# Attention and a token mixer on one core: the quarter-product form of the first mixer product for three groups of tokens instead of two, with the mixer's work spread thinner over attention

## The chip, the cores and the metric

The kernel runs on one core of one Trainium2 chip. The metric is the device time of one execution in microseconds (us). Several executions are timed; the time quoted is their median. A profile is one execution recorded instruction by instruction; its engines are TensorE (PE, and PEld for its weight loads), VectorE (DVE), ScalarE (ACT), GpSimd (POOL) and SyncE (SP, which only issues transfers). A line such as L650 is a line of the kernel's source.

## The reference

```python
# attention: batch 8, heads 8, sequence 576, head dimension 64
scores = q @ k^T / 8
cum    = cumsum(max(s, 0))                     # per batch and head
scores = where(causal, -1e9, scores + min(-(cum_row - cum_col), 0))
attn   = softmax(scores)
x      = (attn @ v)                            # as [batch, 576, 512]
# mixer over the sequence, of rank 32, and over the channels
u   = x + (x^T @ U @ V)^T
out = u + max(u @ w_ch1, 0) @ w_ch2            # 512 -> 2048 -> 512
```

Inputs and outputs are float32; the kernel multiplies in bfloat16 and accumulates in float32.

## The kernel before

**Attention.** The 64 (batch, head) pairs are taken two at a time, so there are 32 head pairs n, four for each batch b. For a head pair, `transposes` (L317) turns q and k on TensorE and copies them into one of a few `slot` tiles; `scores` (L404) makes the transposed scores in `pscore` banks, ScalarE takes the exponential into a `pT` tile (L419, L430), VectorE masks the diagonal (L349); `values` (L464) multiplies by v, and VectorE divides by the row sums into `x_sb` (L473, L474). From batch 2 on, SP also transposes x_sb into xT by a transfer (L481).

**Sequence mixer.** When a batch's four pairs are done, `seqmix` makes u for it. It is a chain between TensorE and VectorE: x by U (L493), a copy to uxT (L502), a transpose (L506), a copy to ux (L508), ux by V for the first 512 tokens (L538) and for the last 64 (L563). VectorE then adds xT and writes u transposed into the tiles `uT` (L518, up to seven pieces).

**Channel mixer.** The 4608 tokens of all batches are cut into nine groups g of 512, so a group reaches over two batches: group 6 is complete with batch 6, groups 7 and 8 only with batch 7, the last. `chanmix(g)` makes the first product `hidden` (L650): 16 steps of four matmuls of 512 columns, each followed by a ReLU on ScalarE into hT (L1018). Then `outputs_by_quarters` makes the second product with seven quarter products instead of eight (Strassen's scheme in Winograd's form): seven products of two times eight matmuls of 256 columns (L699), sums of the weights made once, sums of quarters of hT (`total` L677, the first of them by `first_sums`), and additions into the output tiles (L713). From group NG - 3 = 6 on, `outputs_by_quarters` uses fewer PSUM banks of its own (`quarter`, tags y and z), which exist only in the tail.

**Weaving.** TensorE's order is the order of the program. A list `fill` holds generators of mixer work; `step_fill` takes one unit (for the products, mostly four matmuls of L650 or eight of L699) whenever the counter `pace[0]` passes 16, and `pace[1]` is added at every step of attention. The pace is 12 of 16 from batch 3 to 5 and 10 of 16 after. `chanmix(b - 1)` joins the list in the second head pair of batch b, right after seqmix(b - 1). When group 6's first product is finished, `step_fill` does nothing until the tail's PSUM pools exist. VectorE's, ScalarE's and SP's order after batch 0 is decided by the scheduler, except that weight sums are held behind the VectorE instruction recorded ahead of them (`placed`).

**Tail.** After attention, groups 7 and 8 take the quarter-product form for the first product too: `hidden_by_quarters` (L929) needs sums of the weights w1 (`first_weight_sums`, eight VectorE instructions at L899) and of u (`token_sums`, L911 to L914). Four sets e of seven products of 2x2 matmuls of 256 columns are made per group, with copies and ReLUs on ScalarE (L965, L976, L979, L983, L944, L948) and additions on VectorE (L942). The weight sums lie in the slots that attention leaves free, so they can't be made before its last pairs; here they are stepped one by one inside group 6's `chanmix`. The second product of the group before is woven in by hand: the tuple `fills` says after which step how many units run. The last sequence mixer, seqmix(7), is run by this loop, whose `fill_with` calls place first-product units of group 6 between its steps:

```python
if b == B:
    fill_with(3)
    for _ in range(3):
        step(mixing)
        fill_with(2)
...
for _ in mixing:
    fill_with(1)
```

Of the kernel before, what the change touches and what calls it, by code (L numbers as in the profile page):

```python
# [13 lines left out]
BF16 = mybir.dt.bfloat16  # L14
# [25 lines left out]
def kernel(  # L40
# [17 lines left out]
    DM = H * D  # L58
# [6 lines left out]
    PB = NP // B  # L65
# [2 lines left out]
    KA = D + 4  # L68
    NF = FF // 128
    FT = 2  # L70

    consts = ctx.enter_context(tc.tile_pool(name="consts", bufs=1))
    loads = ctx.enter_context(tc.tile_pool(name="loads", bufs=2))
# [50 lines left out]
    def ones(ap):  # L124
        nc.vector.memset(ap.bitcast(mybir.dt.uint32), 0x3F803F80)

    busy = consts.tile([128, 512], BF16)
    ones(busy)

    alloc_qk(0)  # L130
# [4 lines left out]
    load_qk(0, 4, 2)  # L135
    load_qk(0, 6, 2)

    sel = consts.tile([128, 516], BF16)
    nc.vector.memset(sel, 0.0)
    nc.gpsimd.affine_select(  # L140
        out=sel,
# [102 lines left out]

    w1_sb = consts.tile([128, 4, FF], BF16)
    w2_sb = consts.tile([128, NF, DM], BF16)
    HF, HD = NF // 2, DM // 2
    B11, B21, B22 = w2_sb[:, :HF, :HD], w2_sb[:, HF:, :HD], w2_sb[:, HF:, HD:]
    B12 = w2_sb[:, :HF, HD:]
    B_1, B_2, B_4 = (consts.tile([128, HF, HD], BF16, name=f"w2_sum{i}") for i in (1, 2, 4))  # L250
    B_3 = B12

    def weight_sums():
# [29 lines left out]

    def uT(g):
        if g not in uT_of:
            uT_of[g] = work.tile([128, 4, 512], BF16, tag="uT", name="uT", bufs=3)
        return uT_of[g]


# [299 lines left out]
        for j, pv in enumerate(pvs):  # L589
            nc.vector.tensor_copy(vt[:, j, :, 0:D], pv.rearrange("p (h d) -> p h d", h=H))  # L590

    ux_first = work.tile([128, PB, 128], BF16, tag="ux_first", name="ux_first", bufs=1)

    def mix_first(dt, copy):
        x_sb = x_of[0]
# [89 lines left out]
    def outputs_by_quarters(g, hT, u_sd):  # L685
# [324 lines left out]
    def chanmix(g, hT=None, done=0):  # L1010
        u = uT_of.pop(g)
        if g > 0:
            hT = work.tile([128, NF, 512], BF16, tag="hT", name="hT")
            sums = {1: weight_sums, NG - 3: first_weight_sums}.get(g, lambda: iter(()))()
        for nf in range(done, NF):
            f1 = pwork()
            hidden(f1, u, nf, range(4))
            nc.scalar.activation(hT[:, nf, :], f1, RELU)  # L1018
            if g > 0:
                next(sums, None)  # L1020
            if g > 0 and nf in (12, 14):
                first_sums(hT, nf == 12)
            if nf == (3 if g > 0 else NF - 1):
                u_sd = by_token(u)
            if nf == NF - 1:
                expanded.append(g)
            yield
        if g > 0:
            yield from outputs_by_quarters(g, hT, u_sd)
            return  # L1030
        ahead = {}
        if g == 0:
            for i in range(2):
                ahead[i] = pwork()
                for _ in outputs(ahead[i], hT, i, range(8)):
                    yield
                yield
        for i in range(4):
            f2 = ahead[i] if i in ahead else pwork()
            for _ in outputs(f2, hT, i, range(8 if i in ahead else 0, NF)):  # L1040
                yield
            o_sb = work.tile([128, DM], FP32, tag="o_sb", name="o_sb", bufs=3)
            nc.vector.tensor_tensor(
                o_sb.rearrange("p (a b) -> p a b", a=4),
                f2.rearrange("p (a b) -> p a b", a=4),
                u_sd[:, :, i, :],
                op=ALU.add,
            )
            nc.sync.dma_start(out=out_flat[ds(g * 512 + i * 128, 128), :], in_=o_sb)
            yield  # L1050
# [165 lines left out]
    for n in range(2 * PB, NP + 2):  # L1216
# [36 lines left out]
    tail_sums = {}  # L1253
    tail_sums[NG - 2] = token_sums(
        uT(NG - 2), v_slots[1].rearrange("p a b c -> p (a b c)")
    )
    xT_again = work.tile([128, 4, 640], BF16, tag="xT", name="xT", bufs=1)
    def hidden_plain(u, hT, nfs):
        for at, nf in enumerate(nfs):
            f1 = pwork()  # L1260
# [1 line left out]
            nc.scalar.activation(hT[:, nf, :], f1, RELU)  # L1262
            yield

    for g, sets, fills in ((NG - 2, 4, (0, 0, 2, 4, 6, 8, 10, 12, 14, 17, 20, 23, 25, 26)), (NG - 1, 4, (1, 3, 5, 7, 9, 11, 13, 16, 19, 22, 25, 25, 26, 26))):
        u = uT_of.pop(g)
        u_sd = by_token(u, True)
        hT = work.tile([128, NF, 512], BF16, tag="hT", name="hT")
        for at, _ in enumerate(hidden_by_quarters(u, tail_sums[g], hT, sets)):
            for _ in range(fills.count(at)):  # L1270
                step_fill()
            if at == 3 and g < NG - 1:
                tail_sums[NG - 1] = token_sums(
                    uT(NG - 1), xT_again.rearrange("p a b -> p (a b)")
                )
        if sets < 4:
            for one in (True, False):
                first_sums(hT, one)
# [36 lines left out]
```

## Time and profile before

| | |
|---|---|
| time, median of 3 runs | 363.01 us (362.35 to 363.12) |
| span of the profiled execution, first to last instruction | 362.1 us |
| TensorE busy | 350.2 us, 97% |
| VectorE busy | 276.5 us, 76% |
| ScalarE busy | 213.0 us, 59% |
| first products, L650 | 401 recorded matmuls of 512 columns |
| TensorE's granted clock, mean | 1.000 |

The span covers the instructions; the listed times of the runs are up to 1.0 us longer, which is what lies around them. A row of the timeline gives the start from the span's start, the length, the engine, the line, and the tiles as output<-inputs; the length of a matmul includes its pipeline, so what one costs in a stream is read from the distance of starts. A few matmul records are missing from the trace, so counts can fall one short. In a row of the windows the columns are the window, its length, then busy time and number of instructions of PE, PEld, DVE, ACT and POOL, the granted clock, the share of the transfer engines and GB/s.

### The profile page before, as it was taken

To read this page: it belongs to the slowest core of one execution; us is meant where nothing else is said; L and a number is where in the kernel's file an instruction comes from. 1 tells how busy PE (TensorE), PEld (TensorE's weight loads), DVE (VectorE), ACT (ScalarE), POOL (GpSimd) and SP (SyncE) were. 2 spreads that over 40 slices of the span, in tenths; PEclk is the share of its full clock that TensorE was granted. 3 is DMA by queue.
4 is the path that set the end of the run, shared out by engine and by line. 5 is a ranking of instruction groups with operands and counts; after the bars stand their busy time and mean duration, and the time that the engine had idled before them with its cause. 6 is when DMAs were issued, how large, how long until landed. Compare 5 with 4: busy or idle time off the path is not lost.

```text
span 362.1 us, 9616 instructions
## 1 busy us (share of the span) xinstructions
PE 350.2 (97%) x3999; PEld 256.7 (71%) x4039; DVE 276.5 (76%) x605; ACT 213.0 (59%) x322; POOL 84.7 (23%) x108
## 2 busy tenths in 40 slices
PE   8999999999998999999999999999899999999996
PEld 3676566665587667876688667876488548888885
DVE  8776776778788758995699659986697769676674
ACT  3875975846761678347843676348743554675710
POOL 8997261714040403140214013000000000000000
PEclk9999999999999999999999999999999999999999
DMA  7999999999999899969994999255022716010022
GB/s 104 169 198 204 150 174 129 152 150 143 98 109 114 147 121 70 97 94 126 128 91 72 127 150 91 51 123 79 4 38 70 143 24 125 29 60 31 30 89 87
DMA packets 155123, 37.94 MB, mean 105 GB/s; under 512 B 138696, under 2 KB 153448, under 8 KB 155080
## 3 DMA queue, kind: packets, MB, share of 16 engines
q0 software_dynamic: 110016, 18.50, 82.6%
q1 hardware_dynamic: 44776, 18.64, 31.4%
q8 instruction: 31, 0.51, 0.6%
q10 hardware_dynamic: 288, 0.20, 0.2%
q14 instruction: 12, 0.10, 0.1%
HBM read 37.25 MB, written 9.70 MB: 130 GB/s over the span
## 4 chain that ended last, share of the span: by engine, by line
PE 76%; DVE 11%; ACT 4%; DMA 4%; issue 3%; POOL 1%; DVEq 0%; ACTq 0%; POOLq 0%
PE pwork L650 21%; PE pwork L699 11%; PE pscore L404 9%; PE quarter L699 9%; PE pwork L464 7%; PE parts L929 6%; PE pwork L317 4%; PE pwork L660 3%; DMA xT<-x_sb 2%; DVE slot L677 2%; DVE uT L518 2%; ACT hT L1018 2%; DVE o_sb L713 2%; DMA k_sd<-in_k_dram 2%; ACT pT L419 1%
## 5 line engine op out<-in xcount | busy, mean ns | idle before, releaser
L650 PE MATMUL pwork<-uT,w_sb 128*128 128x512 bf16 x401 | 105.9, 379 | 2.6 <-ACT hT L1018 0.9
L1018 ACT ACTIVATE hT<-pwork 128x512 bf16<-128x512 f32 x108 | 65.2, 608 | 38.4 <-PE pwork L650 38.2
L419 ACT ACTIVATE pT<-pscore 128x1024 bf16<-128x1024 f32 x56 | 56.5, 1029 | 49.8 <-PE pscore L404 49.0
L650 PEld LDWEIGHTS <-w_sb 128*128 128x128 bf16 x448 | 38.3, 98 | 35.9 <-issue 1.3
L404 PE MATMUL pscore<-slot 68*128 68x320 bf16 (+1 forms) x500 | 55.2, 246 | 0.2
L404 PEld LDWEIGHTS <-slot 68*128 68x128 bf16 x564 | 41.2, 97 | 16.9 <-issue 1.3
L699 PEld LDWEIGHTS <-hT 128*128 128x128 bf16 x496 | 46.3, 98 | 7.0 <-DVE uT L518 0.5
L188 POOL DMA_DIRECT2D v_slot<-in_v_dram x36 | 30.3, 855 | 77.6 <-PE pwork L464 65.9
L349 DVE TENSOR_TENSOR pT<-pT,keep 128x512 bf16<-128x512 bf16 (+1 forms) x81 | 28.6, 354 | 21.8 <-ACT pT L419 16.0
L337 DVE COPY slot<-pwork 64x576 bf16<-64x576 bf16 x76 | 34.4, 453 | 4.6 <-PE pwork L317 3.7
L464 PEld LDWEIGHTS <-pT 128*128 128x128 bf16 x870 | 32.4, 98 | 6.9 <-issue 1.8
L464 PE MATMUL pwork<-v_slot,pT 128*128 128x65 bf16 x870 | 35.5, 193 | 1.2 <-DVE uT L518 1.2
L474 DVE TENSOR_TENSOR x_sb<-pwork,rec 128x320 bf16<-128x320 f32 x64 | 31.2, 488 | 1.4
L430 ACT ACTIVATE pT<-pscore 128x1024 bf16<-128x1024 f32 x29 | 30.2, 1043 | 1.7 <-PE pscore L404 1.5
L699 PE MATMUL pwork<-w_sb,hT 128*128 128x256 bf16 x240 | 30.6, 273 | 0.0
L340 DVE COPY slot<-pwork 64x576 bf16<-64x576 bf16 x29 | 23.3, 802 | 5.4 <-PE pwork L317 3.6
L699 PEld LDWEIGHTS <-slot 128*128 128x128 bf16 x256 | 24.1, 98 | 4.6 <-issue 1.6
L114 POOL DMA_DIRECT2D q_sd<-in_q_dram x6 | 12.6, 2105 | 47.2 <-PE pwork L317 34.5
L473 DVE RECIPROCAL rec<-pwork 128x5 f32<-128x5 f32 x64 | 12.0, 190 | 12.3 <-PE pwork L464 12.1
L699 PE MATMUL pwork<-w_sum,slot 128*128 128x256 bf16 x160 | 20.3, 272 | 0.7 <-DVE o_sb L713 0.7
L317 PEld LDWEIGHTS <-q_sd 72*128 72x128 bf16 x256 | 14.7, 98 | 8.8 <-DMA q_sd<-in_q_dram 1.0
L699 PE MATMUL quarter<-w_sb,hT 128*128 128x256 bf16 x144 | 18.0, 273 | 0.3 <-DVE uT L518 0.3
(165 smaller groups left out, 544.4 us busy)
## 6 DMA issues: line engine op xcount, KB each, us to landing
out_dram<-o_sb SPq DMA_DIRECT2D x34, 256.0 KB
w_sb<-in_moe_w_ch_dram POOLq DMA_DIRECT2D x4, 1024.0 KB, 14.3
v_slot<-in_v_dram POOLq DMA_DIRECT2D x28, 128.0 KB, 8.3
q_sd<-in_q_dram POOLq DMA_DIRECT2D x5, 576.0 KB, 15.6
k_sd<-in_k_dram POOLq DMA_DIRECT2D x5, 576.0 KB, 21.8
q_sd<-in_q_dram POOLq DMA_DIRECT2D x4, 288.0 KB, 13.2
k_sd<-in_k_dram POOLq DMA_DIRECT2D x4, 288.0 KB, 13.5
q_sd<-in_q_dram POOLq DMA_DIRECT2D x4, 144.0 KB, 5.2
```

The costliest lines, as they stand in the source:

```text
L188: nc.gpsimd.dma_start(out=vt[:rows_t, t, :, 0:D], in_=v[b, :, ds(t * 128, rows_t), :].rearrange("h p d -> p h d"),)
L317: nc.tensor.transpose(tps[hh][:, c, t2, :], src[:, 2 * hp + hh, ds(t2 * 128, 128)], identity[:TP, :TP],)
L337: copies(n, hh, par)(by_run[:, :, :, par, :], src)
L349: nc.vector.tensor_tensor(dst, dst, keep[:, :, 0:w].to_broadcast([128, n_tiles, w]), op=ALU.min)
L404: nc.tensor.matmul(dst, lhsT=slot[0:KA, hh, ds(S + j * 128, 128)], rhs=slot[0:KA, hh, lo:hi], start=True, stop=True,)
L419: nc.scalar.activation(pT[:, hh, 0:1024], near, EXP, scale=scale)
L430: nc.scalar.activation(pT[:, :, 1024:1536], mid.rearrange("p (a b) -> p a b", a=2), EXP, scale=scale)
L464: nc.tensor.matmul(po[:, i, :], lhsT=pT[:, hh, ds(place(j, i), 128)], rhs=vt[:, j, h, :], start=(j == 0), stop=(j == i), skip_group_check= ...
L474: nc.vector.tensor_tensor(x_sb[:, hp, :, ds(hh * D, D)], po[:, :, 0:D], rec.to_broadcast([128, 5, D]), op=ALU.mult,)
L650: nc.tensor.matmul(f1, lhsT=w1_sb[:, kt, ds(nf * 128, 128)], rhs=u[:, kt, :], start=(kt == 0), stop=(kt == 3),)
L699: nc.tensor.matmul(acc[:, i, :], lhsT=a[:, kt, ds(i * 128, 128)], rhs=b[:, kt, :], start=(begin and i == 0 and kt == 0), stop=(kt == HF - ...
L1018: nc.scalar.activation(hT[:, nf, :], f1, RELU)
```

## The change

A name GL = NG - 4 = 5 is introduced. The groups after GL, that is 6, 7 and 8, take the quarter-product form of the first product in the tail; `chanmix` runs for groups up to 5 in attention. Group 5's second product moves to the tail's form of `outputs_by_quarters`, and `step_fill` now stops when group 5's first product is finished. The pace is 9 of 16 throughout from batch 3 on. The eight weight sums of w1 are made after the attention loop, one before each of eight calls of `step_fill`. The uT tiles are four, not three; to make room, three small tiles of the start (`busy`, `sel`, `ux_first`) are placed inside the tiles that later hold the sums of w2.

```diff
+    GL = NG - 4
...
-    busy = consts.tile([128, 512], BF16)
+    HF, HD = NF // 2, DM // 2
+    B_1, B_2, B_4 = (consts.tile([128, HF, HD], BF16, name=f"w2_sum{i}") for i in (1, 2, 4))
+    busy = B_1.rearrange("p k n -> p (k n)")[:, 0:512]
...
-    sel = consts.tile([128, 516], BF16)
+    sel = B_2.rearrange("p k n -> p (k n)")[:, 0:516]
...
-            uT_of[g] = work.tile([128, 4, 512], BF16, tag="uT", name="uT", bufs=3)
+            uT_of[g] = work.tile([128, 4, 512], BF16, tag="uT", name="uT", bufs=4)
...
-    ux_first = work.tile([128, PB, 128], BF16, tag="ux_first", name="ux_first", bufs=1)
+    ux_first = B_4.rearrange("p k n -> p (k n)")[:, 0:512].rearrange("p (a b) -> p a b", a=PB)
...
-            if g < NG - 3:
+            if g < GL:
...
-        if g >= NG - 3:
+        if g >= GL:
...
-            sums = {1: weight_sums, NG - 3: first_weight_sums}.get(g, lambda: iter(()))()
+            sums = weight_sums() if g == 1 else iter(())
...
-        if NG - 3 in expanded and not ps_tail:
+        if GL in expanded and not ps_tail:
...
-            fill.append(chanmix(b - 1))
-            pace[1] = 12 if b < 6 else 10
+            if b - 1 <= GL:
+                fill.append(chanmix(b - 1))
+            pace[1] = 9
...
     pace[1] = 16
-    while NG - 3 not in expanded:
+    sums = first_weight_sums()
+    for _ in sums:
+        step_fill()
+    while GL not in expanded:
         step_fill()
...
-    tail_sums[NG - 2] = token_sums(
-        uT(NG - 2), v_slots[1].rearrange("p a b c -> p (a b c)")
-    )
+    sum_tiles = [v_slots[1].rearrange("p a b c -> p (a b c)")]
+    tail_sums = {GL + 1: token_sums(uT(GL + 1), sum_tiles[0])}
     xT_again = work.tile([128, 4, 640], BF16, tag="xT", name="xT", bufs=1)
+    sum_tiles.append(xT_again.rearrange("p a b -> p (a b)"))
...
-    for g, sets, fills in ((NG - 2, 4, (0, 0, 2, ...)), (NG - 1, 4, (1, 3, 5, ...))):
+    sets = 4
+    for g in range(GL + 1, NG):
+        if g == GL + 1:
+            fills = (0, 0, 2, 4, 6, 8, 10, 12, 14, 17, 20, 23, 25, 26)
+        else:
+            fills = (1, 3, 5, 7, 9, 11, 13, 16, 19, 22, 25, 25, 26, 26)
...
-                tail_sums[NG - 1] = token_sums(
-                    uT(NG - 1), xT_again.rearrange("p a b -> p (a b)")
-                )
+                tail_sums[g + 1] = token_sums(uT(g + 1), sum_tiles[(g - GL) % 2])
```

More of the change, by code (lines that the diff above doesn't have):

```diff
@@ L246 @@
     w2_sb = consts.tile([128, NF, DM], BF16)
-    HF, HD = NF // 2, DM // 2
     B11, B21, B22 = w2_sb[:, :HF, :HD], w2_sb[:, HF:, :HD], w2_sb[:, HF:, HD:]
     B12 = w2_sb[:, :HF, HD:]
-    B_1, B_2, B_4 = (consts.tile([128, HF, HD], BF16, name=f"w2_sum{i}") for i in (1, 2, 4))
     B_3 = B12
@@ L1252 @@
     ps_t = ctx.enter_context(tc.tile_pool(name="ps_t", bufs=4, space=bass.MemoryType.PSUM))
-    tail_sums = {}
-    tail_sums[NG - 2] = token_sums(
-        uT(NG - 2), v_slots[1].rearrange("p a b c -> p (a b c)")
-    )
+    sum_tiles = [v_slots[1].rearrange("p a b c -> p (a b c)")]
+    tail_sums = {GL + 1: token_sums(uT(GL + 1), sum_tiles[0])}
     xT_again = work.tile([128, 4, 640], BF16, tag="xT", name="xT", bufs=1)
+    sum_tiles.append(xT_again.rearrange("p a b -> p (a b)"))
     def hidden_plain(u, hT, nfs):
@@ L1263, in hidden_plain @@
             yield
-    for g, sets, fills in ((NG - 2, 4, (0, 0, 2, 4, 6, 8, 10, 12, 14, 17, 20, 23, 25, 26)), (NG - 1, 4, (1, 3, 5, 7, 9, 11, 13, 16, 19, 22, 25, 25, 26, 26))):
+    sets = 4
[4 more added lines that the diff above has]
+            fills = (1, 3, 5, 7, 9, 11, 13, 16, 19, 22, 25, 25, 26, 26)
         u = uT_of.pop(g)
```

## The prediction

> **What bounds the kernel now.** I read the page first (busy time, slices, chain), then the windows by stage, then the timeline of TensorE and of VectorE around the place where attention hands over to the mixer's tail.
>
> ```profile
> PE 350.2 (97%) x3999; PEld 256.7 (71%) x4039; DVE 276.5 (76%) x605; ACT 213.0 (59%) x322; POOL 84.7 (23%) x108
> ...
> PEclk9999999999999999999999999999999999999999
> ...
> PE 76%; DVE 11%; ACT 4%; DMA 4%; issue 3%; POOL 1%; DVEq 0%; ACTq 0%; POOLq 0%
> ```
>
> TensorE is busy for 97% of the span, at full clock throughout, and it carries 76% of the chain that ended last. So a matmul saved is worth its spacing in the stream, as long as no wait takes its place.
>
> The windows (length, then busy time of PE, PEld, DVE, ACT, POOL) show how much room the other engines have:
>
> ```profile
> 221.00:240.00 19.00, 18.59 (x251) 16.39 (x250) 18.26 (x42) 6.70 (x11) 0.00 (x0) 1.00 0.58 66
> 240.00:263.00 23.00, 21.82 (x251) 13.46 (x254) 15.75 (x41) 17.41 (x29) 0.00 (x0) 1.00 0.37 62
> 321.00:346.00 25.00, 25.00 (x230) 22.26 (x229) 17.22 (x28) 15.37 (x25) 0.00 (x0) 1.00 0.11 38
> ```
>
> Where attention is woven with second products (221 to 240) VectorE is at 96%; where it is woven with first products (240 to 263) ScalarE is at 76% and TensorE idles 1.2 us; in the tail (321 to 346) TensorE never idles. Over 122 to 281 TensorE's idle time adds up to 2.7 us.
>
> The handover, TensorE's timeline (start, us, then the instructions):
>
> ```profile
> 289.13 0.65 PE L493 MATMUL pwork<-U_sb,x_sb 128*128 128x32 bf16 x20
> 289.64 1.89 PE L650 MATMUL pwork<-uT,w_sb 128*128 128x512 bf16 x8
> 291.36 0.22 PE L506 MATMUL pwork<-identity,uxT 128*128 128x128 bf16 x1
> 291.42 1.89 PE L650 MATMUL pwork<-uT,w_sb 128*128 128x512 bf16 x7
> 293.24 0.39 PE L538 MATMUL pscore<-V_sb,ux 32*128 32x512 bf16 x2
> ...
> 293.57 2.76 PE L650 MATMUL pwork<-uT,w_sb 128*128 128x512 bf16 x12
> 296.44 0.29 PE L563 MATMUL pwork<-V_end,ux 128*128 128x64 bf16 x4
> 296.57 0.60 PE L929 MATMUL parts<-uT,w_sb 128*128 128x256 bf16 x4
> 297.44 1.92 PE L699 MATMUL quarter<-w_sb,hT 128*128 128x256 bf16 x16 [0.26 <-DVE uT L518]
> 299.19 0.60 PE L929 MATMUL parts<-v_slot,slot 128*128 128x256 bf16 x4
> ```
>
> And VectorE's:
>
> ```profile
> 281.50 2.49 DVE L899 TENSOR_TENSOR slot<-w_sb 128x1024 bf16<-128x1024 bf16 x4
> ...
> 286.11 0.49 DVE L474 TENSOR_TENSOR x_sb<-pwork,rec 128x320 bf16<-128x320 f32 x1
> ...
> 291.62 0.29 DVE L508 CAST ux<-pwork 128x128 bf16<-128x128 f32 x1 [1.50 <-PE pwork L506]
> ...
> 294.44 1.28 DVE L518 TENSOR_TENSOR uT<-pscore,xT 128x128 bf16<-128x128 f32 x2
> 295.64 1.74 DVE L518 TENSOR_TENSOR uT<-pwork,xT 128x64 bf16<-128x64 f32 x5
> ```
>
> The reader is to see that the last sequence mixer (L493, L506, L538, L563) is a chain of round trips to VectorE, and that 27 wide matmuls of L650 are shown inside it as cover (44 from 285.68 on, by the built order); and that VectorE makes its eight weight sums (L899) under that cover, from 281.5 to 288.4.
>
> **The sum, part by part.** *The products.* Group 6 goes from 64 matmuls of 512 columns to 7x4x4 = 112 of 256; the built programs differ by exactly these 48. Wide ones: eight from 289.64 to 291.36, 0.2155 us each, so 64 take 13.79. Narrow ones: sixteen from 297.44 to 299.19, 0.109 each, so 112 take 12.2. Saved: **1.6 us** on TensorE, all of it on the path.
>
> Here a rule speaks against the change. The Trainium skill's page "TensorE: Matmul & The Clock Gate", section "Back-to-back issue gap", gives about 131 ns a matmul for 512 columns in a real stream with weight loads and 81 for 128; its isolated formula is columns over 2.4 GHz plus 2.5 ns. By the stream figures, with an estimate of 98 ns between them for 256, 64 cost 8.4 us and 112 cost 10.9, a loss of 2.6. The rows above go by the isolated formula, weight loads included, so I keep the gain.
>
> *The handover.* In the built order of the new kernel group 5's first product is used up too early: nine units of four wide matmuls run ahead of attention's last values, one between the two heads, two after them, then TensorE has L493, L506, L538, L563 with nothing between, and then the tail. VectorE's order behind them is: seven pieces of L518, all eight L899, the second half of one token total (L677), one add of L942, the first o_sb of group 5 (L713). TensorE's waits in that order: the first L929 on the pair's pieces of L518, the first L699 on the last piece, the next L929 on the first two L899, a later one on six of them, and the third kind of quarter product (A_2 by B_2) on that o_sb. I put zero where the last values matmuls have streamed (285.68 in the old trace) and use the old rows:
> - x_sb is done at 1.25 (0.92 in the old trace, plus 0.33 for a token sum that now stands between). xT's transfer: its packets ended at 289.42, 2.8 after the x_sb of 286.60; with issue and semaphore, 4.3 here.
> - Eight wide matmuls to 1.73, L493 (0.51) to 2.24. VectorE then has two token sums and a total first, uxT ends at 2.85; L506 at 2.95; ux (0.26 after it starts, 0.29 long, as at 291.36 and 291.62) ends at 3.55; L538 and L563 to 4.1.
> - L518 starts when xT is there, 4.35; the pair is done 1.28 later, all 2.94 later (294.44 to 297.38). So the first L929 goes at 5.7 and the first sixteen L699 at 7.35, ending 9.1.
> - Eight L899, 0.60 apart (four in 2.49), end at 12.1; three more at 0.60 end at 13.9. A_2 by B_2 can start at **14.0**.
> - What TensorE streams up to there: 1.72 + 0.51 + 0.06 + 0.33 + 0.12 + 0.44 + 1.75 + five eights of 0.87 = 9.3. Lost: 4.7 us.
>
> The old trace loses in the same stretch: 303.56 - 285.68 = 17.9 against 17.0 streamed, 0.85. Net 3.9; and VectorE, which was 3 us ahead there, now starts the tail level: its next eleven instructions (7x0.60 + 4x0.33 = 5.5) stand against six eights (5.2), 0.3 more. **Cost 4.2 us.** Bounds: 2.0 if xT, evacuation and sums overlap better than their order says (only the idle before the first L699 remains), 5.5 if VectorE stays late through the group, which at 17.22 of 25 us busy it need not.
>
> A slow clock could follow such idling. The trace shows half speed only at its start: nine matmuls of 512 columns in 4.02 us, 0.43 each, where 0.2155 each would make 1.9. In its middle, 1.1 us without a matmul (256.7 to 257.8) left the spacing at 0.215; the idle stretches reckoned here are 1.6 and 1.2 us. So I take nothing, and 2.0 us as the upper bound, one such start. The same page, section "What's actually happening", has the clock fall to half after an idle window of some 3.4 us; by that too nothing is lost unless the stretches count as one.
>
> *Attention with 9 units in 16 steps, not 12 or 10.* About 4.5 units per head pair, not 6 or 5. TensorE per pair: 2.9 (16 L317, 18 of L404, 30 L464 at their spacings) plus 4.5x0.87 = 6.8, against 8.0 seen at pace 12 and 7.1 at pace 10. The moved units themselves cost the same in the tail. What changes is cover. The slices at pace 10 (221 to 281) idle 1.6 us in 60, those at pace 12 (122 to 221) 1.0 in 99, and 0.9 of the former is one wait of L650 for L1018 where a sequence mixer fell among first products. In the new order two of five fall so (b = 4, 5), in the old one such; the stage is some 26 us shorter. I take **0**: bounds -1.5 (over half the idle goes) and +3 (next part).
>
> *At nothing.* Group 5's second products take the tail's form: seven wide adds on VectorE, not eleven; the matmuls are the same. Its sends and u_sd transposes stand in SP's order behind the same xT transposes. The third tail group's x_sb is the one that group 6 leaves, 24 us before it is read. The DMA issues on POOL come earlier with attention: q and k for the next batch landed 18 us before use (218.5 for 236.8), a batch of four pairs gets some 6 us shorter, so this cover holds; without it, each us late is one lost. The fourth uT only adds memory. The shared tiles: last read by matmuls at about 21 (busy), 20 (sel) and 34 us (ux_first), first sum at 77.
>
> Sum: -1.6 + 4.2 + 0 = +2.6. The span was 362.1 and the median of the runs 363.0, 0.9 lies around the span: 364.7 in the span, **365.7 us** as a time.
>
> **Rivals.** *Attention gives back more than the handover takes* (the faster side): with fewer units VectorE falls below saturation in the second-product stretches and ScalarE in the others, and TensorE's 2.7 us of idle there, and the small gaps beside it, go. For it: 96% on VectorE. Against: TensorE lost only 0.4 us in that very window. At the handover's lower bound: -1.6 + 2.0 - 1.5 = -1.1, 361.9. It decides from where attention's gain passes the handover's cost less 1.6.
>
> *VectorE becomes attention's bound.* Per pair it needs about 3.3 us at its spacings, 0.8 for its share of the sequence mixer, and 0.74 per second-product unit: 4.5 units make 7.4 against TensorE's 7.1 with its mixer share. Over some 12 such pairs 3.6 us: 369.3. Against: the lag is caught up among first products, as now.
>
> *The clock falls at the handover:* 365.7 + 2.0 = 367.7. Against: the idle stretches are short.
>
> **How the numbers follow.** The forecast has 0.6, the faster rival 0.15, VectorE 0.15, clock 0.1. The range reaches from the faster rival's time to the VectorE rival's, 361.9 to 369.3. No change means within 0.2% (0.7 us), about what a measurement of this kernel can tell: faster 0.17 (the faster rival and a rest of the forecast), same 0.08, slower 0.75.
>
> **What would show it.** Right: L929 at about 0.109 spacing in three groups, L650 with 64 fewer; at the handover a wait of TensorE of over 1 us on uT L518 and waits on the sums' line, the clock at 1.00. Wrong: no idle there, or idle spread over attention, or VectorE's second-product windows at 100% with TensorE below 95%.

## The result, and the profile after

The changed kernel is slower: 374.85 us (median of six runs, 373.33 to 379.58) against 363.05 us for the kernel before on the same chip, a ratio of 1.030 with a 95% interval of 1.026 to 1.035. The forecast was 365.7 us, with a range up to 369.3. The profiled execution, the quickest, took 373.33 us with a span of 371.6; the others had a mean granted clock as low as its 0.995 or lower (down to 0.976), and the ratio leaves out two of them, of 379.2 and 379.6 us, that fell into a slower state of the chip. In the changed kernel the lines named here are numbered one higher than before: L651 is the wide first product, L700 the second product, L930 the quarter form of the first, L519 the writing of u, L900 makes the weight sums, and L678 and L714 are what L677 and L713 were.

The page of the changed kernel, with the busy times, the clock in 40 slices and the chain that ended last:

```profile
PE 355.9 (96%) x4087; PEld 263.4 (71%) x4087; DVE 281.2 (76%) x617; ACT 217.6 (59%) x329; POOL 85.0 (23%) x108
...
PEclk9999999999999999999999999999998999999999
...
PE 64%; DVE 15%; ACT 9%; DMA 6%; issue 4%; SPq 1%; ACTq 0%; DVEq 0%
```

TensorE's share of the chain fell from 76% to 64%, VectorE's and ScalarE's rose by 4 and 5 points, and one slice has a clock below full. The windows of the changed kernel (length, then PE, PEld, DVE, ACT, POOL, granted clock) say in which stages:

```profile
221.00:240.00 19.00, 18.17 (x235) 12.30 (x233) 14.17 (x36) 14.69 (x24) 0.00 (x0) 1.00 0.11 22
240.00:258.00 18.00, 17.11 (x240) 14.87 (x237) 16.09 (x37) 6.89 (x10) 0.00 (x0) 1.00 0.47 93
273.00:279.00 6.00, 3.85 (x54) 2.20 (x52) 6.00 (x17) 1.79 (x3) 0.00 (x0) 1.00 0.51 30
279.00:289.00 10.00, 8.93 (x65) 7.23 (x66) 10.00 (x21) 2.77 (x5) 0.00 (x0) 0.83 0.28 53
289.00:312.00 23.00, 23.00 (x213) 20.57 (x211) 18.91 (x33) 15.11 (x24) 0.00 (x0) 1.00 0.14 47
```

From 273 to 289, the handover, VectorE is busy without a gap and TensorE idles 3.2 us; from 289 on TensorE is full again. In attention TensorE idles some 5% in both kinds of stretch (0.8 us of 19 beside first products, 0.9 of 18 beside second ones; before, 1.2 of 23 and 0.4 of 19), although VectorE is busy for 75% of the first stretch and 89% of the second, ScalarE for 77% and 38%.

Where the time went can be counted at one mark, the prediction's zero: the start of the wide matmuls right behind attention's last values. It moved from 285.68 to 273.62 us, 12.06 earlier. But 112 quarter matmuls of group 5 (12.2 us) and 28 wide ones (6.03) fewer stand ahead of it, so it should have come 18.2 earlier: attention lost **6.2 us**. Behind the mark the span grew by 21.56, and the work there by 16.65 (two times 112 narrow matmuls more, 24.4, and 36 wide ones fewer, 7.76): handover and tail lost **4.9 us**. Less the products' 1.6, which are reckoned here from the same distances of starts, this is the growth of the span, 9.5.

The handover on TensorE in the changed kernel (start, length, instruction, and in brackets the wait):

```profile
273.62 1.89 PE L651 MATMUL pwork<-uT,w_sb 128*128 128x512 bf16 x8
275.34 0.66 PE L494 MATMUL pwork<-U_sb,x_sb 128*128 128x32 bf16 x20
276.62 0.23 PE L507 MATMUL pwork<-identity,uxT 128*128 128x128 bf16 x1 [0.62 <-DVE uxT L503]
277.24 0.39 PE L539 MATMUL pscore<-V_sb,ux 32*128 32x512 bf16 x2 [0.39 <-DVE ux L509]
...
279.04 0.61 PE L930 MATMUL parts<-uT,w_sb 128*128 128x256 bf16 x4 [1.18 <-DVE uT L519]
280.68 2.95 PE L700 MATMUL quarter<-w_sb,hT 128*128 128x256 bf16 x16 [1.04 <-DVE uT L519]
283.43 1.06 PE L930 MATMUL parts<-v_slot,slot 128*128 128x256 bf16 x4
...
288.46 1.04 PE L700 MATMUL quarter<-w_sum,slot 128*128 128x256 bf16 x8
```

The first L930 stands at zero + 5.4 and the sixteen L700 at zero + 7.1 (predicted 5.7 and 7.35). But these sixteen need 2.75 us to the next start, not 1.75, and the last row, A_2 by B_2, starts at zero + 14.84 without a wait. The same kernel's granted clock, microsecond by microsecond, shows why:

```profile
280.00:281.00 1.00, 0.32 (x3) 0.29 (x3) 1.00 (x3) 0.31 (x1) 0.00 (x0) 1.00 0.01 3
281.00:282.00 1.00, 1.00 (x9) 0.77 (x7) 1.00 (x3) 0.00 (x0) 0.00 (x0) 0.68 1.09 209
282.00:283.00 1.00, 1.00 (x6) 0.70 (x5) 1.00 (x3) 0.00 (x0) 0.00 (x0) 0.50 1.16 217
283.00:284.00 1.00, 1.00 (x6) 0.75 (x5) 1.00 (x3) 0.00 (x0) 0.00 (x0) 0.50 0.52 96
284.00:285.00 1.00, 1.00 (x8) 0.73 (x7) 1.00 (x3) 0.00 (x0) 0.00 (x0) 0.61 0.00 0
```

For some 3.4 us TensorE ran at half speed, just when its work had come: 0.32 + 0.50 + 0.50 + 0.39 = 1.7 us. VectorE in the same stretch of the changed kernel:

```profile
277.70 1.28 DVE L519 TENSOR_TENSOR uT<-pscore,xT 128x128 bf16<-128x128 f32 x2
278.90 1.73 DVE L519 TENSOR_TENSOR uT<-pwork,xT 128x64 bf16<-128x64 f32 x5
280.55 2.48 DVE L900 TENSOR_TENSOR slot<-w_sb 128x1024 bf16<-128x1024 bf16 x4
...
286.57 0.68 DVE L714 TENSOR_TENSOR o_sb<-quarter,u_sd 128x512 f32<-128x512 f32 x1
```

The order is the predicted one: u, the weight sums, then the first o_sb, which ends at 287.25. TensorE, slowed by its clock, came to the product that needs it only at 288.46, so the waits that were predicted behind the sums did not happen; the half clock stood in their place. Without its 1.7 us TensorE would have come at about 286.8 (an estimate), half a microsecond before that end.

The list of TensorE's waits in attention of the changed kernel (86 to 273 us: waiter, tile, releaser, then total us, times, longest):

```profile
PE pwork L651 <- ACT hT L1019: 1.8, 2, 0.9
PE pwork L494 <- DVE x_sb L475: 1.1, 2, 0.6
PE pwork L651 <- DVE x_sb L475: 1.0, 4, 0.4
PE pwork L700 <- DVE x_sb L475: 0.8, 2, 0.5
PE pwork L651 <- DVE o_sb L714: 0.6, 1, 0.6
PE pwork L465 <- DVE uT L519: 0.5, 1, 0.5
```

The same list of the kernel before (86 to 285 us):

```profile
PE pwork L464 <- DVE uT L518: 1.2, 1, 1.2
PE pwork L650 <- ACT hT L1018: 0.9, 1, 0.9
PE pwork L699 <- DVE o_sb L713: 0.7, 2, 0.4
PE pwork L650 <- DVE x_sb L474: 0.2, 1, 0.2
```

Only the first and the last two kinds have a counterpart of any size there. The products do not read x_sb, so their waits on it are for a PSUM bank: it still holds values that VectorE has not divided and copied out. L494 does read x_sb: of its two waits the first (0.6 us) is for the bank that it writes, the second (0.5) for the last head pair's values themselves.

### The profile page after: what moved, and what is told of

Its sections match the earlier page's. It is cut to its first block, busy times and chain, and to the rows that moved or that the text cites. A ratio compares the mean times of both kernels' runs of the same rounds, so it can differ in the third digit from the quotient of the medians.

```text
span 371.6 us, 9775 instructions
## 1 busy us (share of the span) xinstructions
PE 355.9 (96%) x4087; PEld 263.4 (71%) x4087; DVE 281.2 (76%) x617; ACT 217.6 (59%) x329; POOL 85.0 (23%) x108
## 4 chain that ended last, share of the span: by engine, by line
PE 64%; DVE 15%; ACT 9%; DMA 6%; issue 4%; SPq 1%; ACTq 0%; DVEq 0%
PE pwork L651 14%; PE quarter L700 13%; PE parts L930 9%; PE pwork L700 7%; PE pscore L405 6%; PE pwork L465 4%; DMA xT<-x_sb 4%; ACT pT L420 4%; PE pwork L661 3%; PE pwork L318 3%; ACT hT L1019 3%; DVE o_sb L714 2%; DVE uT L519 2%; DVE slot L678 2%; ACT pT L431 2%
## 5 line engine op out<-in xcount | busy, mean ns | idle before, releaser
L651 PE MATMUL pwork<-uT,w_sb 128*128 128x512 bf16 x368 | 91.9, 379 | 3.7 <-ACT hT L1019 1.8
L1019 ACT ACTIVATE hT<-pwork 128x512 bf16<-128x512 f32 x92 | 55.7, 611 | 35.6 <-PE pwork L651 35.3
L651 PEld LDWEIGHTS <-w_sb 128*128 128x128 bf16 x384 | 33.1, 98 | 34.4 <-issue 3.6
L405 PE MATMUL pscore<-slot 68*128 68x320 bf16 (+1 forms) x500 | 53.4, 246 | 0.5 <-DMA slot<-hT 0.3
L700 PEld LDWEIGHTS <-hT 128*128 128x128 bf16 x496 | 47.2, 99 | 9.2 <-issue 1.7
L465 PE MATMUL pwork<-v_slot,pT 128*128 128x65 bf16 x870 | 34.1, 194 | 0.6 <-DVE uT L519 0.5
L700 PEld LDWEIGHTS <-slot 128*128 128x128 bf16 x256 | 24.0, 98 | 3.9 <-issue 0.7
L700 PE MATMUL quarter<-w_sb,hT 128*128 128x256 bf16 x192 | 25.3, 280 | 1.0 <-DVE uT L519 1.0
L700 PE MATMUL pwork<-w_sb,hT 128*128 128x256 bf16 x192 | 24.6, 273 | 0.5 <-DVE x_sb L475 0.4
L943 DVE TENSOR_TENSOR hT<-pT,parts 128x512 bf16<-128x512 f32 x24 | 16.2, 684 | 9.9 <-PE parts L930 7.1
```

The source lines that it names most:

```text
L405: nc.tensor.matmul(dst, lhsT=slot[0:KA, hh, ds(S + j * 128, 128)], rhs=slot[0:KA, hh, lo:hi], start=True, stop=True,)
L465: nc.tensor.matmul(po[:, i, :], lhsT=pT[:, hh, ds(place(j, i), 128)], rhs=vt[:, j, h, :], start=(j == 0), stop=(j == i), skip_group_check= ...
L651: nc.tensor.matmul(f1, lhsT=w1_sb[:, kt, ds(nf * 128, 128)], rhs=u[:, kt, :], start=(kt == 0), stop=(kt == 3),)
L700: nc.tensor.matmul(acc[:, i, :], lhsT=a[:, kt, ds(i * 128, 128)], rhs=b[:, kt, :], start=(begin and i == 0 and kt == 0), stop=(kt == HF - ...
```

## Experiments: which part costs what

Five kernels. The first four ran beside the kernel before at a median of 363.25 us, the last on another chip.

**The pace alone.** In the kernel before:

```diff
-            pace[1] = 12 if b < 6 else 10
+            pace[1] = 9
```

> The kernel before, with the pace of 9 from batch 3 on and nothing else of the change: two groups in the tail, the old weight sums inside group 6's first product, and the work that attention leaves over run densely around seqmix(7). Theory 1 (thin cover: with 4.5 units per head pair TensorE waits for PSUM banks and sequence mixers inside attention): about 5 us slower than before, 368, and the idle time of TensorE up to the last values matmul is about 11 us as in the changed kernel, against 6 before. Rival (attention's extra idle comes from something else in the change, such as the fourth uT or the moved sums): 363, no change.

370.78 us, ratio 1.021 (1.019 to 1.023), clock 1.000. Most of the loss is in this one number, which the prediction had priced at nothing. TensorE's waits in its attention are those of the changed kernel to within 0.3 us in each row.

**Units kept for the last sequence mixer.** In the changed kernel, whose fill_with calls ran in both rounds of the last batch:

```diff
-        if b == B:
+        if n == NP + 1:
             fill_with(3)
```

> The changed kernel, but the nine units of group 5's first product that ran ahead of the last values matmuls are kept for the loop's last round, where they lie between the steps of seqmix(7). Theory 1 (the handover loses its time because seqmix(7) has no matmuls between its steps): some 4.5 us faster than the changed kernel, 369.3; the granted clock stays at 1.00; q16 of group 5 follows the first L930 without a wait of over 0.5 us. Rival (the eight weight sums on VectorE hold the tail back, wherever the units lie): at most 1 us faster, 373.

372.32 us, ratio 1.027 (1.023 to 1.030), clock 0.998 to 1.000: 1.3 us better by the ratios (1.7 by the spans of the profiled executions), not 4.5, and nearer to the rival's 1 us. Its list of waits from 266 to 300 us names what is late next:

```profile
PE quarter L700 <- DVE o_sb L714: 1.7, 2, 0.9
PE quarter L700 <- DVE uT L519: 0.6, 1, 0.6
```

With the last sequence mixer covered and the clock held, TensorE meets the o_sb additions that queue behind the eight weight sums.

**Dummy matmuls.** Thirteen matmuls of no use placed in the handover of the changed kernel:

```diff
+                if hp == 1:
+                    spin((3, 2, 0)[at], warm)
...
+        if n == NP + 1:
+            spin(8, warm)
```

> The changed kernel with 13 dummy matmuls of 512 columns into a free PSUM bank: three after L494, two after L507, eight after L564 of seqmix(7). They add no work that anything waits for and keep TensorE streaming in most of its idle time at the handover. Theory 1 (the idle stretch makes the clock fall, and sixteen L700 then take 2.75 us in place of 1.75): clock 1.00 in all windows, 0.8 to 1.4 us faster than the changed kernel, 372.5 to 373. Rival (VectorE's chain of L519, eight sums and three more sets the start of A_2 by B_2 whatever TensorE's clock does): no gain, the windows show clock 1.00 and TensorE waits longer on o_sb L714.

373.33 us (372.77 to 376.69), ratio 1.030 (1.026 to 1.035). The clock held at the handover. The profiled execution is 3.9 us late by a dip of the clock at its start, its mark at 277.51 us, so the stretch that was 279 to 289 is this one:

```profile
282.90:292.90 10.00, 8.90 (x76) 7.05 (x74) 10.00 (x21) 2.77 (x5) 0.00 (x0) 1.00 0.28 52
```

Yet the three runs with a clock of 0.999 or more took 372.8 to 373.7, hardly less than the changed kernel's quickest. VectorE and TensorE in this run:

```profile
282.11 0.68 DVE L678 TENSOR_TENSOR hT<-hT 128x1024 bf16<-128x1024 bf16 x1
282.71 1.28 DVE L519 TENSOR_TENSOR uT<-pscore,xT 128x128 bf16<-128x128 f32 x2
...
290.98 0.68 DVE L714 TENSOR_TENSOR o_sb<-quarter,u_sd 128x512 f32<-128x512 f32 x1
291.83 1.04 PE L700 MATMUL quarter<-w_sum,slot 128*128 128x256 bf16 x8
```

Here two more sums of quarters (L678) stand ahead of L519 in VectorE's order, and u is ready 1.1 us later: the first L930 starts at the mark + 6.5, not 5.4. A_2 by B_2 starts at the mark + 14.3, not 14.8, right behind the o_sb that ends at 291.66. So of the clock's 1.7 us half a microsecond came back. At full clock it is VectorE's chain of u, weight sums and o_sb that TensorE follows, and neither the clock nor the sums alone are worth their own size.

**Weight sums early.** In the changed kernel:

```diff
-            sums = weight_sums() if g == 1 else iter(())
+            sums = {1: weight_sums, GL: first_weight_sums}.get(g, lambda: iter(()))()
...
-    sums = first_weight_sums()
-    for _ in sums:
-        step_fill()
```

> The changed kernel with the eight weight sums stepped inside group 5's first product (as the kernel before had them inside group 6's), so VectorE makes them ahead of seqmix(7) and not behind it. Theory 1 (the missing cover of seqmix(7) is the cost; the sums lie behind matmuls for the most part): 0 to 1 us faster, 373. Rival (VectorE's 4.8 us of sums are the cost): 4 us or more faster, 369.5.

377.72 us (373.98 to 380.19), ratio 1.035 (1.029 to 1.041), at clocks of 0.972 to 0.995: no gain; its run at 0.995 took 373.98, where the changed kernel's two at 0.995 took 373.33 and 373.80. With nothing beside the last sequence mixer TensorE waits for u as before (0.6, 0.4, 1.2 and 0.6 us), and the clock falls again, in the profiled execution for 6.8 us, from 282.5 to 289.3, twice as long as in the changed kernel. What the sums alone are worth does not show beside it.

**Both.** The two edits above together:

> The changed kernel with both edits at the handover together: nine first-product units kept for the last sequence mixer, and the eight weight sums made inside group 5's channel mixer. Theory (two waits stand side by side at the handover, so that taking away one only shows the other): with both gone the handover costs what it cost in the kernel before, and what is left is the thin pace less the 1.6 us of the products: 370.8 - 1.6 = 369.2, with no wait of TensorE over 0.7 us between 275 and 290 us. Rival one (the waits that stayed when the units alone were held back do not come from the weight sums): 372.3 as there. Rival two (seven products of 256 columns save nothing over four of 512): 370.8, the time of the thin pace alone.

369.06 us (368.11 to 369.54), ratio 1.016 (1.013 to 1.019) to 362.84 us on that chip, as expected, at clocks of 0.998 or more. One wait is left from 266 to 300 us, 0.6 us of L700 on uT L519, where the kernel before waits for 0.26. So the handover costs little once both covers are there, and what remains is about the pace less the products.

## Experiments: why a thinner pace costs time

The first three ran beside a kernel before at 362.84 us.

**Pace 10 throughout.** In the kernel before:

```diff
-            pace[1] = 12 if b < 6 else 10
+            pace[1] = 10
```

> The kernel before with the pace at 10 of 16 from batch 3 on, not 12 and then 10. Theory A (the amount of mixer work beside attention counts): 9 of 16 throughout cost 7.5 us, and 10 removes a bit more than half as many units as 9 does, so 366.5 to 367.5. Theory B (the order counts: at 9 of 16 the places without a unit drift until values and transposes follow each other with nothing between, while at 10 of 16 each set of values is followed by a unit in every head pair): 363.3 to 364.0, with hardly a wait of L650 on the copy L474 in attention.

368.56 us, ratio 1.016 (1.012 to 1.019): above both expectations. Batches 3 to 5 (from the first values matmul of batch 3 to that of batch 6) took 105.8 us against 111.1 with twelve units fewer (10.5 us of work), so 5.2 were lost there. At 9 of 16 the changed kernel took 101.2 us for them with eighteen fewer (15.7), so it lost 5.8. Most of the cost comes with the first units taken away.

**Pace 9 with the units placed.** In the kernel with the pace alone:

```diff
+        thin = pace[1] == 9
...
+            pace[1] = 8 if thin else pace[1]
             for at, _ in enumerate(transposes(n + 1)):
...
+            pace[1] = 6 if thin else pace[1]
             for at, _ in enumerate(scores(n, pT_of(n))):
...
+            pace[1] = 16 if thin else pace[1]
             run(values(n - 1, pT_of(n - 1)))
```

> The kernel before with a thin pace again, 9 of 16 on the average, but with the units put at fixed places: 16 of 16 at the steps of values, 8 at those of transposes, 6 at those of scores. The amount of mixer work beside attention is that of the thin pace alone (370.8), only its order differs: each of the two steps of values has a unit behind it. Theory A (the amount counts): 370 to 371. Theory B (the order counts): the waits of L650 on L474 behind values and transposes go, TensorE's idle time in attention falls from 11.7 us to about 6, 364.5 to 366.

370.5 us, ratio 1.019 (1.016 to 1.022), against 370.78: this order brings nothing back. But the waits of L650 on ScalarE went and those on x_sb shrank, and another took their place; the first row of its list of waits, 114 to 275 us, and the row of VectorE that it waited for:

```profile
PE pwork L464 <- DVE uT L518: 3.2, 2, 3.0
...
183.20 1.09 DVE L518 TENSOR_TENSOR uT<-pwork,xT 128x256 bf16<-128x256 f32 x3 [4.15 <-DMA xT<-x_sb]
```

Once, a transfer of xT came late; TensorE stood for 3.0 us, and then its clock was at half from 184.6 to 188.0. Three of the four runs have that clock, 0.995; the fourth, at 0.999, took 368.55. So whether the order counts, with the transfers in time, is not settled.

**One unit ahead of L538**, in the kernel before:

```diff
+        if hp == 1 and FT < b < B:
+            fill_with(1)
+            for at, _ in enumerate(mixing):
+                if at < 3:
+                    fill_with(1)
```

> The kernel before, with a first- or second-product unit put ahead of L538 of the sequence mixer inside attention and one fewer left behind it; the units that join there are the same. Theory: the wait of 1.3 us of the next unit on ScalarE's ReLU after three units in a row (once in the kernel before) goes: 362.0 to 362.3. Rival: the unit used up earlier is missed elsewhere, or the wait was already hidden by the evacuation: 363.2.

363.53 us against 362.84, ratio 1.002 (0.999 to 1.004): no gain. The wait on ScalarE and those on o_sb went from its list, and 1.0 us of L464 on uT is left, as in the kernel before (1.2). Where that time went instead is not settled.

**Plain copies.** The next eight kernels share this edit, and the first is their own kernel before:

```diff
-                nc.sync.dma_start_transpose(
-                    out=xT_of[b][:, hp, :].rearrange("p (t m) -> p t m", t=5),
+                nc.sync.dma_start(
+                    out=xT_of[b][:, hp, :],
...
-        nc.sync.dma_start_transpose(
-            out=u_sd.rearrange("p a b c -> p (a b) c"), in_=u.rearrange("p a b -> p (a b)")
+        nc.sync.dma_start(
+            out=u_sd.rearrange("p a b c -> p (a b c)"), in_=u.rearrange("p a b -> p (a b)")
```

> The kernel before, with the transposing transfers of x_sb (L481) and of u (L1005) replaced by plain copies of the same sizes, so the transposition is left out and u holds other numbers. This and the next three kernels share that edit and are compared with each other. It may be a little quicker where xT or u_sd came late, which is hardly ever: 362.0 to 363.0.

362.8 us, ratio 0.999 (0.996 to 1.003): the transposing transfers cost nothing there that these runs can tell. This trace has no missing matmuls, and its list of waits from 114 to 285 us is short:

```profile
PE pwork L650 <- ACT hT L1018: 0.9, 1, 0.9
PE pwork L699 <- DVE o_sb L713: 0.7, 2, 0.4
PE pwork L464 <- DVE uT L518: 0.2, 1, 0.2
```

With `pace[1] = 9` added:

> The thin pace alone (9 of 16 from batch 3 on), with plain copies in place of the transposing transfers. If the transfers play no part in what the thin pace costs, the difference to the kernel before with plain copies is again 7.5 us: 369.5 to 370.5. If attention at the thin pace waits for xT, the difference falls by what those waits were, to 5 or less.

369.51 us, ratio 1.016 (1.010 to 1.022): 6.7 us over the line above, so the thin pace costs the same without transposing transfers. Its waits are those of the changed kernel's list to within 0.3 us in each row. VectorE was busy 81.24 of 101 us in batches 3 to 5, 80%, against 86.47 of 111.5, 78%: it is not full. One of the waits, on TensorE's timeline of this run:

```profile
165.67 0.29 PE L317 MATMUL pwork<-identity,k_sd 72*128 72x72 bf16 x4
166.23 1.04 PE L650 MATMUL pwork<-uT,w_sb 128*128 128x512 bf16 x4 [0.28 <-DVE x_sb L474]
```

and VectorE's timeline ahead of it:

```profile
164.27 0.48 DVE L474 TENSOR_TENSOR x_sb<-pwork,rec 128x320 bf16<-128x320 f32 x1
164.67 0.68 DVE L713 TENSOR_TENSOR o_sb<-U,u_sd 128x512 f32<-128x512 f32 x1
165.27 0.18 DVE L473 RECIPROCAL rec<-pwork 128x5 f32<-128x5 f32 x1
165.37 0.41 DVE L337 COPY slot<-pwork 64x576 bf16<-64x576 bf16 x1
165.70 0.47 DVE L474 TENSOR_TENSOR x_sb<-pwork,rec 128x320 bf16<-128x320 f32 x1
```

VectorE is busy at that place without a gap: o_sb additions of the second product stand between and ahead of the copies that free the banks. ScalarE does the same to its ReLU; its timeline in this run, where L650 waits 0.91 us and starts at 178.69:

```profile
176.19 1.04 ACT L419 ACTIVATE pT<-pscore 128x1024 bf16<-128x1024 f32 x1
177.09 1.05 ACT L430 ACTIVATE pT<-pscore 128x1024 bf16<-128x1024 f32 x1
178.00 0.64 ACT L1018 ACTIVATE hT<-pwork 128x512 bf16<-128x512 f32 x1
```

**Sums left out.** Two kernels, at the thin and at the old pace, lighten VectorE by sums of quarters:

```diff
-            total(A_3, A11, A21, ALU.subtract, i)
...
-            total(A_4, A12, A_2, ALU.subtract, i)
...
-            product(p3, A_4, B22, i)
+            product(p3, A_2, B22, i)
```

> As the thin pace with plain copies, and two of the four sums of quarters (A_3 and A_4 at L677) left out for the groups whose second product lies in attention; the product that would use A_4 uses A_2. That takes four VectorE instructions of 0.68 us, 2.7 us, out of each group; 24 of them, 16.2 us of VectorE, lie between 130 and 256 us in the trace of the thin pace. TensorE's work is unchanged. Theory V (with little mixer work beside it TensorE overtakes VectorE, and what it waits for is VectorE's queue): most of the 7.5 us comes back, 4 us or more under the thin pace with plain copies. Theory C (it is the length of the chain of a head pair or of a sequence mixer, which a shorter queue hardly changes): under 1.5 us.

368.34 us, ratio 1.012 (1.007 to 1.018), 1.2 less than with them.

> The control: the kernel before with plain copies and the same two sums left out. Theory V: at 12 of 16 VectorE holds TensorE less, so a gain of 0.5 to 1.5 us against the kernel before with plain copies, far less than on the thin pace. Theory C: within 0.5 us of it.

361.48 us, ratio 0.993 (0.990 to 0.997), 1.3 less. The gain is about the same at both paces, so theory V, a general load of VectorE, falls as it was put; theory C expected no gain in the control, and there is one. The lists of waits say that the two gains are different ones: at the thin pace only the wait of L493 on x_sb shrank, from 1.1 us to 0.2, and in the control that of L699 on o_sb went, 0.7.

**Additions left out.** Two more lighten it by additions:

```diff
-        add(o, o, p2)
...
-        add(o12, o12, p3)
...
-            if i == 0:
-                add_u(o22, o22, 1, 1)
...
-        add(U2, U2, p7)
...
-        add(o21, o21, p4)
```

> The thin pace with plain copies (369.5), and five of the eleven o_sb adds of a second product in attention (L713) left out: those of the second, third and fourth bank, one of u and one of U2, 0.68 us each. In the trace of the thin pace the waits of TensorE on x_sb have such an add ahead of L474 in VectorE's queue. Theory V2 (the adds in the queue are what TensorE meets when it arrives early): these waits add up to some 4.5 us, and most go: 365 to 366.5. Theory C (the chain itself, reciprocal, product, copies, is too long for the thin cover): 368 to 369.5. The kernel before has 1 us of such waits, so the control can gain about 1 by them.

365.95 us, ratio 1.010 (1.007 to 1.013). (L1018 is L1012 in this kernel.) Three kinds of wait are left in its attention, 114 to 273 us:

```profile
PE pwork L650 <- ACT hT L1012: 1.8, 2, 0.9
PE pwork L493 <- DVE x_sb L474: 1.1, 2, 0.6
PE pwork L650 <- DVE x_sb L474: 0.6, 2, 0.4
```

> The control: the kernel before with plain copies (362.8) and the same five adds left out. Theory V2: 361.5 to 362.3, since its waits on o_sb and x_sb are about 1 us. Theory C: 362.3 to 362.8.

361.66 us, ratio 0.997 (0.993 to 1.000). By medians the additions are worth 3.6 us at the thin pace and 1.1 in the kernel before; by the ratios, which compare each with the runs beside it, 2.2 and 1.1. So the queue of additions is a part of the pace's cost, 1.1 to 2.4 us of the 6.7, and theory V2 holds for that part only. The intervals of these ratios are 1 to 2 us wide to either side, so the size of this part is rough.

**Additions out and a unit ahead of L538**, the last two edits together at the thin pace:

> As the thin pace with plain copies and the five adds left out, and in addition one unit put ahead of L538 in every sequence mixer inside attention, so that two units follow it, not three. In the trace of the thin pace L650 waits there twice for ScalarE's L1018, which stands behind two exponentials: 1.3 us each where 0.3 is the least. If these are a second, separate part of the cost, 1.5 to 2 us under the run with the adds left out; if the unit is missed elsewhere, as in the kernel before, no change.

364.89 us, ratio 1.006 (1.004 to 1.008): 1.1 less again (1.4 by the ratios), where the same move gained nothing in the kernel before. Both rows of ScalarE's wait are gone from the list; the two rows on x_sb stay. Against the control with the additions out, 3.2 us of the pace's cost are still there (3.3 by the ratios); a control with the unit moved as well was not run.

**The waits counted by starts.** The lists show less than a wait costs: they count from the end of the last matmul's pipeline, and leave out what is under 0.15 us. In TensorE's rows above, the four L317 from 165.67 on have a length of 0.29 us but take 0.13 in a stream, so the wait that ends at 166.23 costs 0.43 us and not 0.28. Counted like this (distance to the next start, less the usual distance in a stream), from the sequence mixer of batch 2, where the pace is set, to the mark, in us (gaps that are only a missing matmul record, whose weight load is there, are left out):

| TensorE waits for | before, plain copies | pace 9, plain copies | before, additions out | pace 9, additions out, unit moved |
|---|---|---|---|---|
| hT, by ScalarE | 1.3 | 2.6 | 1.3 | 0.9 |
| pT of L436, by ScalarE | 0 | 1.1 | 0 | 1.0 |
| x_sb, before products | 0 | 2.5 | 0 | 0.9 |
| x_sb, before L493 | 0 | 1.7 | 0 | 1.7 |
| o_sb | 1.0 | 1.0 | 0 | 0 |
| uT and ux | 0.6 | 0.6 | 0.2 | 0.5 |
| sum | 2.9 | 9.5 | 1.5 | 5.0 |

The first two differ by 6.5 us, of the 6.7 that the thin pace lost between these two places. So nearly the whole cost stands in waits of TensorE for banks and data that VectorE (4.2 us more) and ScalarE (2.4 more) give late. The last two differ by 3.4, where the medians differ by 3.2 and the two profiled executions by 4.1.

**The other direction.** In the kernel before with plain copies, more cover late:

```diff
-        if b == B:
+        if n == NP + 1:
             fill_with(3)
...
-            pace[1] = 12 if b < 6 else 10
+            pace[1] = 12
```

> The kernel before with plain copies (362.8), the pace at 12 of 16 to the end, not 10 from batch 6 on, and the nine units of fill_with kept for the round of the last sequence mixer, so that this has as much between its steps as now. If thin cover costs batch 6 and the last pairs what it costs batches 3 to 5 at 10 of 16 (some 1.7 us a batch), 360.5 to 361.5. If the old pace of 10 there is already free of waits but for the one of 1.3 us on ScalarE, 361.5 to 362.8.

362.31 us, ratio 0.998 (0.996 to 1.000), beside 0.999 (0.996 to 1.003) for plain copies alone: half a microsecond at best, within what these runs can tell. No version that does all the work beats the kernel before by more than that.

## Why the prediction was wrong

The direction was right, the size and the range were not. The miss against the profiled execution is 373.33 - 365.7 = 7.6 us: 6.2 in attention, 0.7 at the handover and in the tail, and the rest around the span. The 1.5 us from there to the median go with lower granted clocks; where in those runs the clock was low is not known, since one execution alone has a profile.

- **The step that failed: "Attention with 9 units in 16 steps, not 12 or 10", of which it says "I take 0", with bounds of -1.5 and +3.** It cost 6.2 us in the changed kernel and 6.7 to 7.5 alone. The reckoning compared idle time of stretches at pace 10 and at 12 inside one trace and found 1.6 us in 60 against 1.0 in 99. Those at pace 10 lie late in attention; ten throughout then lost 5.2 us in batches 3 to 5. Counted by starts, TensorE's waits grew from 2.9 to 9.5 us when the pace alone was changed, with plain copies. Idle time "spread over attention" was one of the prediction's own signs of being wrong. Its sum said that TensorE needs 7.1 us a pair at pace 9, with its share of the sequence mixer, and VectorE 7.4 in the second-product stretches; it should have asked of each wait how much earlier TensorE would arrive and what stands ahead in the queue of the engine that frees the bank.
- **The rival "VectorE becomes attention's bound"** named one of the two engines, with the wrong mechanism and half the price (3.6). VectorE is 80% busy. It is late in places, where additions and sums stand ahead of the copy of the values, and ScalarE is late behind its exponentials. The additions and the exponentials' wait, taken away, gave 3.6 to 4.6 us at the thin pace, against 1.1 for the additions in the control. The 3.2 us that stayed are seen as waits in the trace but were not all taken away: half of them is L493 on x_sb (1.7 us), where sums of quarters stand in VectorE's queue, and with two of these sums left out its row in the list went from 1.1 to 0.2.
- **The handover, 4.2 us:** the mechanism, the order and the waits up to the sixteen L700 were right (0.62 + 0.39 + 1.18 + 1.04 us, starts within 0.3 us). The loss to A_2 by B_2 is 14.84 - 9.3 - 0.85 = 4.7, and 4.9 to the end. The step "So I take nothing" for the clock failed: it fell to half for 3.4 us, the upper bound of 2.0 being about its size, 1.7. The wait behind the sums that the sum had instead did not come. That the term was near, 4.2 for 4.9, is luck: two errors nearly cancel.
- **What lies around the span:** 0.9 was taken from a span of one execution and a median of others; in the runs since, time and span of the same execution differ by about 1.7 us. That is 0.8 of the miss. (And 364.7 + 0.9 is 365.6, not 365.7.)
- **The products, -1.6:** not run alone. Four L930 in a stream start 0.44 us apart in the changed kernel (0.109 each), as reckoned, and the kernel with both handover edits is 0.5% (some 2 us) below the pace alone, each by its ratio to the kernel before. The loss of 2.6 us that the stream figures of the Trainium skill's page "TensorE: Matmul & The Clock Gate", section "Back-to-back issue gap", would give would put it above the pace alone. The measurement decides: on this stream, weight loads included, the isolated formula holds.
- **At nothing:** the fourth uT, the shared tiles and the issues on POOL show no wait in the changed kernel's lists, as predicted.

The same page, section "What's actually happening", ties the fall to half speed to an idle window of some 3.4 us, free-running. No wait here was longer than 1.2 us; but from 278 to 281 us TensorE was busy for 0.93 of 3.0, and the clock fell at 281.4 and came back some 3.4 us later. The length agrees with the page's window; that a mostly idle stretch suffices is what the row adds.

## What to carry to other kernels

Work that is woven beside a latency-bound stage is cover, not only load: before thinning it, look at each wait of the thin places, ask what stands ahead in the releasing engine's queue, and bound the cost by a stage that was really run that thin. Where two covers are taken from one place, giving back one may bring little (here 1.3 us and none), and the pair more (5 us by the ratios). A busy share of 80% does not say whether an engine is late at the one instruction that frees a bank. And a wait costs more than its idle time: count it from start to start.

## What the hardware showed that was not expected

The clock fell to half after four gaps of 0.4 to 1.2 us within 5 us, none of which would have been suspected alone, and stayed there for 3.41 us of full work (granted 0.50 in 282 to 284). With the units placed it fell after one wait of 3.0 us, for 3.41 us; with the sums early, at the handover, for 6.83. In some executions it also dipped at the start: the runs with dummy matmuls and with early sums were profiled with such a dip, both from 12.8 to 23.1 us, 10.24 us long (granted 0.84 over 8 to 40 us in the first, which took 3 to 4 us more than its other runs), in a part of the program that their edits do not touch. By the traces' own records of the clock these lengths are one, two and three times 3.41 us.
